# Loading the query weights in four stepped pieces of 16, 16, 32 and 64 partitions

## The chip, the core and the metric

The kernel runs on one core of a Trainium2 chip. The metric is the device time of one execution in microseconds; the figure before is the median of three runs. A core has an on-chip memory (SBUF) of 128 partitions, 16 DMA engines that bring data from HBM, and the engines TensorE (PE), VectorE (DVE), ScalarE (ACT), GpSimd (POOL) and SyncE (SP). SP issues nearly all loads here. Below, one of the 16 DMA engines is called a lane.

## What is computed

One token goes through a layer norm, attention against a cache of 16384 keys in each of 8 key heads (32 query heads, 128 wide), and a small gated network behind it:

```python
def _A_ref(x, k_cache, v_cache, wq, wo):
    q = (x @ wq).reshape(B, Sq, Hq, Dh).transpose(0, 2, 1, 3)
    k = jnp.repeat(k_cache, rep, axis=1)
    v = jnp.repeat(v_cache, rep, axis=1)
    p = softmax(jnp.einsum("bhqd,bhkd->bhqk", q, k) * (Dh ** -0.5))
    o = jnp.einsum("bhqk,bhkd->bhqd", p, v)
    return o.transpose(0, 2, 1, 3).reshape(B, Sq, Hq * Dh) @ wo
...
x = A_x
h = x + _A_ref(_layernorm(x), A_k_cache, A_v_cache, A_wq, A_wo)
h2 = h + _B_ref(_layernorm(h), B_w1, B_w2, B_w3, B_w4)
```

`wq` is 512 x 4096 and `wo` 4096 x 512 in bf16, 4 MB each; the keys and the values are 32 MB each. With a sequence of one token the shifted branch inside `_B_ref` sees zeros only, so that `w1` and `w2` are not read; `w3` and `w4` are.

## The kernel before

The program is written as a list of operations for each engine, in the order in which they are issued; a small planner puts a semaphore wait ahead of an operation whose data, named by keys such as `("v", 0)`, another engine or a load has to deliver. Nothing reorders the list.

Loads are made by `load` (L475), all on SP but that of the token, `x4`, which ACT issues. SP issues them in this order: the query weights `wq`; the keys of the first pair of heads (8 MB); then, each as its buffer comes free, values and keys of the pairs in turn, the last pair's keys in two halves; the output weights `wo`; the weights `w3` and `w4` in four loads; at the end the store of the output. A load of 128 partitions brings one contiguous row of HBM to each partition: 32 KB for `wq` and `wo`, 64 KB for a pair's keys or values.

`wq` is put into the buffer `vb`, which later holds the values, under the key `("v", 0)`. Ahead of its use stand the layer norm's operations on DVE. The last of these, at L630, writes the normalised token `xn`; it waits for `wq` as well, so that the matmuls behind it need to wait for `xn` alone:

```python
dve(lambda e: e.tensor_scalar(xn[:, :], hT[:, :, 0], st[0][:, 0:1], st[0][:, 6:7], ALU.add, ALU.mult),
    r=["hT", (("st", 0), 0), (("st", 0), 6)] + [("v", x) for x in range(VP)], w=["xn"])
```

At L639 PE multiplies `xn` with `wq` in 32 matmuls, one bank of 512 columns after the other. DVE transposes the queries (L646), puts them into `qb` (L653) and copies the pair's part to `qn` (L768). From then on the loop over the four pairs runs: DVE transposes the keys in pieces (L663), PE forms the scores (L674), a softmax follows (L688 to L706), and PE multiplies with the values (L722). Behind the last pair come the output weights (L809), the second layer norm and the network (L832, L858).

The load of the first values reuses `vb`, so that SP waits ahead of it until PE has read `wq`. The load of the next pair's keys waits until DVE has transposed the pair that lay in its buffer. At the end the matmuls at L809 wait for `wo`, and those at L858 for the pieces of `w4`.

Of the kernel before, what the change touches and what calls it, by code (L numbers as in the profile page):

```python
# [350 lines left out]
HQ = 32  # L351
HKV = 8
SK = 16384
DH = 128
REP = HQ // HKV
FM = 1792
NCH = D // 128
FQ = FM // 4
NHC = FM // 128

WO = ((0, 32),)
VP = 1

# [24 lines left out]
def bass_sequential_preLN__gqa_block_cached__mixer_s_mlp__decode_kernel(  # L388
# [13 lines left out]
    with ExitStack() as ctx:  # L402
# [26 lines left out]
        st = [sb(f"st{i}", [128, 16], FP32) for i in range(2)]  # L429
        added = sb("added", [128, 2], FP32)  # L430
        sti = [sb(f"sti{i}", [128, 2, 2], I32) for i in range(2)]
        xn = sb("xn", [128, NCH], BF16)
# [20 lines left out]
        wq_sb, wo_sb = vb, kb[2]  # L453
# [10 lines left out]
        hT = kt[:, 2944:3200].bitcast(FP32).rearrange("p (k u) -> p k u", k=NCH)  # L464
# [9 lines left out]
        def load(name, dst, src, key, by="SP", also=()):  # L474
            P.op(by, lambda e: e.dma_start(dst, src), w=[key, *also], dma=name)  # L475
# [4 lines left out]
        def load_keys(j, y):  # L480
            n = 128 * DH
            if j in WHOLE:
                load("k0", kb_all[:, AT[j] * n:(AT[j] + 2) * n], pair_rows(A_k_cache, j), ("r", AT[j], 0),
                     also=[("r", AT[j] + z, i) for z in range(2) for i in range(1 - z, RPARTS)])
                return
            load(f"half{y}", kb[y][:, :], pair_rows(A_k_cache, j)[:, y * n:(y + 1) * n], ("r", y, 0),
                 also=[("r", y, i) for i in range(1, RPARTS)])
# [19 lines left out]
        def act(fn, r=(), w=(), bank=(), own=None):  # L507
            return P.op("ACT", fn, r, w, bank, own=own)
# [15 lines left out]
        def unread_held(times, at):  # L524
            for _ in range(times):
                P.op("PE", lambda e: held(e, O_ps[1][at:, :], field[:, 0:128 - at], field[:, 0:512], True, True),
                     r=["qb"], bank=[("O", 1)])
# [9 lines left out]
        def piece(cuts, m):  # L537
            return [lo <= m < hi for lo, hi in cuts].index(True)
# [54 lines left out]

        load("x4", x4[:, :], A_x[0, 0:1, :].rearrange("o (q j) -> (o q) j", q=4), "x4", "ACT")
        wq_in = A_wq.rearrange("(p k) c -> p (k c)", k=NCH)
        load("wq", wq_sb[:, 0:NCH * HQ * DH], wq_in[:, :], ("v", 0), also=[("v", x) for x in range(1, VP)])
        load_keys(0, 0)

        dve(lambda e: e.memset(mean4[:, :], -1.0 / (32 * D)), w=["mean4"])
        for n in range(2):  # L600
# [8 lines left out]
            r=["ident_f", "x4"], w=["quarter"])  # L609
# [9 lines left out]
            r=["ident_f"], w=["row32"])  # L619
        dve(lambda e: e.tensor_reduce(maskdd[:, :], ident_f[:, :].rearrange("p (n d) -> p d n", d=4), AX.X, ALU.add),  # L620
            r=["ident_f"], w=["maskdd"])
# [3 lines left out]
        for z, src, key, of, n in ((zo, row32[:, :].rearrange("p (g n h) -> p g h n", g=2, h=REP), "zo", "row32", 4),  # L625
# [3 lines left out]
                src.unsqueeze(3).to_broadcast([128, 2, REP, 4, n]), AX.X, ALU.add), r=[of], w=[key])  # L629
        dve(lambda e: e.tensor_scalar(xn[:, :], hT[:, :, 0], st[0][:, 0:1], st[0][:, 6:7],  # L630
                                      ALU.add, ALU.mult),
            r=["hT", (("st", 0), 0), (("st", 0), 6)] + [("v", x) for x in range(VP)], w=["xn"])

        keys = [("s", 0), ("s", 1), ("O", 0), ("O", 1), "A", "mn", "spare0", "spare1"]
        wq_k = wq_sb[:, 0:NCH * HQ * DH].rearrange("p (k c) -> p k c", k=NCH)
        for i, key in enumerate(keys):
            P.part("query", i)
            for k in range(NCH):
                pe(lambda e, k=k: e.matmul(row[:, bass.ds(P.b + P.b0, 512)], copies(xn[:, k:k + 1], 128),  # L639
                                           wq_k[:, k, bass.ds(P.c + P.c0, REP * DH)], start=(k == 0), stop=(k == NCH - 1)),  # L640
                   r=["xn"], also=[("v", x) for x in range(VP)], w=["n" if key == "mn" else key], bank=[key])
        P.part()
        for g in range(2):
            half = banks[64 * g:64 * g + 64, PAIRS * g:PAIRS * g + PAIRS, :].rearrange("p j c -> p (j c)")
            for b in range(2):
# [3 lines left out]
                    r=["n" if x == "mn" else x for x in keys[PAIRS * g:PAIRS * g + PAIRS]], w=["qcol"],  # L649
                    bank=keys[PAIRS * g:PAIRS * g + PAIRS])  # L650
        for a in range(4):
            lo, hi, at = 32 * a, 32 * a + 32, QPAD + 32 * a
# [137 lines left out]
        act(lambda e: e.activation(scr[0:1, 1:2], mean4[0:1, 0:1], ACTF.Gelu_apprx_tanh), r=["mean4"], w=["scr"])  # L790
        for n, (lo, hi) in enumerate(WO):
            load(f"wo{n}", wo_sb[:, lo * D:hi * D], A_wo.rearrange("(p r) c -> p (r c)", p=128)[:, lo * D:hi * D],
# [5 lines left out]
        for n, (lo, hi) in enumerate(W4):  # L798
# [4 lines left out]
            r=["o_m"], w=["o_f"])  # L803
# [3 lines left out]
        for r_ in range(32):  # L807
# [3 lines left out]
                                              stop=(r_ < 4 or r_ >= 28), skip_group_check=(r_ >= 4)),  # L811
               r=[("r", 2, piece(WO, r_)), "o_b"], w=[("O", 0)], bank=[("O", 0)])
        unread_held(2, 96)
        h_ps, hkey = banks[:, 6, :], "spare0"
        for n in range(2):
            dve(lambda e, n=n: e.tensor_copy(osum[:, 256 * n:256 * n + 256], O_ps[0][:, 256 * n:256 * n + 256]),  # L816
                r=[("O", 0)], w=[("osum", n)], bank=[("O", 0)])
        for q in range(4):
            pe(lambda e, q=q: e.matmul(h_ps[32 * q:32 * q + 32, 0:128], copies(row32[:, 0:1], 32),  # L819
                                       osum[:, q * 128:(q + 1) * 128], start=True, stop=True),  # L820
               r=[("osum", q // 2), "row32"], w=[hkey], bank=[hkey])
# [4 lines left out]
            r=["hT", (S, 0)] + [("r", 0, 0)], w=["hc"])  # L826
# [3 lines left out]
        for k in range(NCH):  # L830
            for q in range(4):
                pe(lambda e, k=k, q=q: e.matmul(s_ps[32 * q:32 * q + 32, 0, 0:FQ], hc[:, k, :],  # L832
                                                w3_sb[:, k, q * FQ:(q + 1) * FQ], start=(k == 0), stop=(k == NCH - 1)),
                   r=["hc"] + [("r", 0, n) for n in (piece(W3, k),) if n], w=[("s", 0)], bank=[("s", 0)])
# [5 lines left out]
            r=["xs", (S, 6), "hr"], w=[hkey], bank=[hkey])  # L840
# [8 lines left out]
        for m in range(NHC):  # L849
# [5 lines left out]
            for o in range(4):  # L855
# [5 lines left out]
                   r=[("r", 0, len(W3) + piece(W4, m)), ("hcol", piece(GELU, m))],  # L861
                   w=[hkey], bank=[hkey])
# [7 lines left out]
             r=[("fin", 0), ("fin", 1)], w=["out"], dma="out")  # L870
# [32 lines left out]
```

## Time and profile before

| what | value |
|---|---|
| median of 3 runs | 189.37 us (189.31 to 189.54) |
| the profiled execution's own time | 189.73 us |
| its span, first to last instruction | 188.3 us |
| mean granted TensorE clock | 0.927 |
| HBM read | 79.17 MB |
| busy share of the span: PE, DVE, ACT, POOL | 70%, 62%, 7%, 2% |

The times of the views count from the first instruction of the span. The profiled execution took 1.43 us more than its span; that lies before the first and behind the last instruction. In the view of the DMA queues a stretch is cut into 40 equal slices. The line `DMA` gives the busy share in tenths and the line `GB/s` the bytes that were moved, and both put a packet wholly into the slice in which it begins; where slices are shorter than a packet takes, a number other than 0 marks a packet's beginning. `q1` is SP's queue and `q10` ACT's.

### The profile page before, as it was taken

To read this page: it belongs to the slowest core of one execution; us is meant where nothing else is said; L and a number is where in the kernel's file an instruction comes from. 1 tells how busy PE (TensorE), PEld (TensorE's weight loads), DVE (VectorE), ACT (ScalarE), POOL (GpSimd) and SP (SyncE) were. 2 spreads that over 40 slices of the span, in tenths; PEclk is the share of its full clock that TensorE was granted. 3 is DMA by queue.
4 is the path that set the end of the run, shared out by engine and by line. 5 is a ranking of instruction groups with operands and counts; after the bars stand their busy time and mean duration, and the time that the engine had idled before them with its cause. 6 is when DMAs were issued, how large, how long until landed. Compare 5 with 4: busy or idle time off the path is not lost.

```text
span 188.3 us, 2390 instructions
## 1 busy us (share of the span) xinstructions
PE 131.2 (70%) x768; PEld 50.0 (27%) x758; DVE 116.1 (62%) x141; ACT 13.8 (7%) x22; POOL 4.6 (2%) x8
## 2 busy tenths in 40 slices
PE   0109900579979913998979309899799989796774
PEld 0103300223322501333324103333235433232221
DVE  5730570999736008999363069994699898633155
ACT  3000200000004000000040000000310000410012
POOL 8100000000000000000000000000000000000000
PEclk9999995589999985599999975999999999999999
DMA  6999999999999999899999999998999999889994
GB/s 223 446 446 446 446 446 446 446 446 446 446 446 432 446 446 432 376 404 404 404 446 446 446 446 446 446 446 369 418 439 446 543 446 432 376 369 418 415 412 158
DMA packets 2175, 79.19 MB, mean 421 GB/s; under 512 B 254, under 2 KB 382, under 8 KB 510
## 3 DMA queue, kind: packets, MB, share of 16 engines
q1 hardware_dynamic: 2166, 79.17, 97.6%
q8 instruction: 1, 0.02, 0.0%
q10 hardware_dynamic: 8, 0.00, 0.0%
HBM read 79.17 MB, written 0.00 MB: 420 GB/s over the span
## 4 chain that ended last, share of the span: by engine, by line
DMA 66%; DVE 22%; PE 10%; issue 1%; SPq 0%; DVEq 0%
DMA kb<-in_A_k_cache_dram 48%; DVE kt L663 19%; DMA kb<-in_A_wo_dram 18%; PE banks L520 3%; PE banks L674 2%; PE banks L722 2%; PE banks L809 1%; DVE mx L688 1%; PE banks L858 1%; DVE kt L846 0%; PE banks L819 0%; SPq L475 0%; PE banks L691 0%; DVE kt L816 0%; PE banks L558 0%
## 5 line engine op out<-in xcount | busy, mean ns | idle before, releaser
L674 PE MATMUL banks<-kt,qn 128*128 x256 | 70.3, 413 | 31.3 <-DVE kt L663 30.3
L663 DVE STREAM_TRANSPOSE kt<-kb 128x2048 int32<-128x2048 int32 (+2 forms) x24 | 70.6, 2994 | 26.6 <-DMA kb<-in_A_k_cache_dram 25.3
L674 PEld LDWEIGHTS banks<-kt,qn 128*128 x256 | 26.1, 102 | 75.5 <-issue 62.4
L520 PE MATMUL banks<-qb 128*128 128x512 bf16 x71 | 26.3, 387 | 0.6
L722 PE MATMUL banks<-vb,pt 128*32 128x512 bf16 x256 | 14.7, 379 | 0.2 <-POOLq L501 0.2
L700 ACT ACTIVATE kt<-banks,bias 128x1024 bf16<-128x1024 f32 x4 | 4.5, 1113 | 132.5 <-DVE nmh L695 132.5
L639 PE MATMUL banks<-vb,xn 128*128 x32 | 9.2, 460 | 7.0 <-DVE xn L630 7.0
L520 PEld LDWEIGHTS banks<-qb 128*128 128x128 bf16 x71 | 6.9, 97 | 19.0 <-issue 18.6
L688 DVE TENSOR_REDUCE mx<-banks 128x1 f32<-128x1024 f32 x4 | 4.9, 1225 | 10.5 <-PE banks L674 10.5
L722 PEld LDWEIGHTS banks<-vb,pt 128*32 128x32 bf16 x256 | 8.6, 97 | 4.5 <-POOLq L501 0.3
L706 DVE STREAM_TRANSPOSE pt<-kt 64x1024 bf16<-64x1024 bf16 x6 | 7.4, 1239 | 3.3 <-ACT kt L700 3.2
L646 DVE STREAM_TRANSPOSE kt<-banks 64x1024 f32<-64x1024 f32 x4 | 4.8, 1227 | 7.4 <-PE banks L639 7.4
L639 PEld LDWEIGHTS banks<-vb,xn 128*128 128x128 bf16 x32 | 3.7, 115 | 12.2 <-issue 9.8
L683 ACT ACTIVATE banks<-mean 128x1024 f32<-128x1024 f32 x4 | 4.1, 1027 | 19.6 <-DVE kt L646 19.5
L691 PE MATMUL banks<-mxd,mean 128*128 128x128 f32 x8 | 2.0, 326 | 4.7 <-DVE mxd L689 4.7
L746 DVE SCALAR_TENSOR_TENSOR od<-banks,rowc,od 128x128 f32<-128x128 f32 x12 | 4.2, 351 | 0.4
L610 PE MATMUL banks<-x,quarter 4*128 4x128 bf16 x1 | 0.3, 282 | 5.4 <-DVE quarter L608 5.4
L816 DVE COPY kt<-banks 128x256 f32<-128x256 f32 x2 | 0.8, 420 | 5.0 <-PE banks L809 5.0
L608 DVE CAST quarter<-ident_f 4x128 bf16<-4x128 f32 x1 | 2.9, 2876 | 1.3 <-DMA x<-in_A_x_dram 1.3
L532 PE MATMUL banks<-qb 128*128 128x512 bf16 (+1 forms) x10 | 3.6, 379 | 0.0
L743 DVE TENSOR_SCALAR od<-banks,rowc 128x128 f32<-128x128 f32 x4 | 1.3, 318 | 3.7 <-PE banks L722 3.7
L751 PE MATMUL banks<-od,zo 128*32 128x128 f32 x10 | 2.0, 283 | 1.9 <-DVE od L746 1.6
(76 smaller groups left out, 44.3 us busy)
## 6 DMA issues: line engine op xcount, KB each, us to landing
kb<-in_A_k_cache_dram SPq DMA_DIRECT2D x2, 4096.0 KB, 31.6
vb<-in_A_wq_dram SPq DMA_DIRECT2D x1, 4096.0 KB, 12.5
kb<-in_A_wo_dram SPq DMA_DIRECT2D x1, 4096.0 KB, 33.8
kb<-in_B_w_dram SPq DMA_DIRECT2D x1, 1792.0 KB, 34.0
kb<-in_B_w_dram SPq DMA_DIRECT2D x1, 1152.0 KB, 36.4
kb<-in_B_w_dram SPq DMA_DIRECT2D x1, 512.0 KB, 37.2
kb<-in_B_w_dram SPq DMA_DIRECT2D x1, 128.0 KB, 37.1
vb<-in_A_v_cache_dram SPq DMA_DIRECT2D x4, 24.3
```

What stands on the lines that cost most here:

```text
L520: P.op("PE", lambda e: e.matmul(O_ps[1][:, :], field[:, 0:128], field[:, 0:512], start=True, stop=True), r=["qb"], bank=[("O", 1)], times= ...
L532: return e.add_instruction(mybir.InstMatmult(name=nc.get_next_instruction_name(), engine=m.engine, ins=m.ins, outs=m.outs, start_tensor_ca ...
L639: pe(lambda e, k=k: e.matmul(row[:, bass.ds(P.b + P.b0, 512)], copies(xn[:, k:k + 1], 128), wq_k[:, k, bass.ds(P.c + P.c0, REP * DH)], sta ...
L646: dve(lambda e, g=g, b=b, half=half: e.transpose(qcol[64 * g:64 * g + 64, 2 * b:2 * b + 2, :, :].rearrange("p e m u -> p (e m u)"), half.r ...
L663: P.op("DVE", lambda e, t=t, n=n: e.transpose(pieces(kt, t, n).bitcast(I32), pieces(kb[at], t, n).bitcast(I32)), r=[("r", at, i) for i in ...
L674: pe(lambda e, n=n: e.matmul(row[:, bass.ds(P.y, 512)], qn[:, n, bass.ds(P.q, 128)], key_piece(P.k, n), start=False, stop=(n == 3), skip_g ...
L683: act(lambda e: e.activation(s_all, copies(mean4[:, 0:1], 1024), ACTF.Identity, scale=0.0), r=["mean4", "p"], w=[("s", 0), ("s", 1)], **both)
L688: dve(lambda e: e.tensor_reduce(mx[:, :], s_all, AX.X, ALU.max), r=[("s", 0), ("s", 1)], w=["mx"], **both)
L700: act(lambda e: e.activation(p_sb[:, :], s_all, ACTF.Exp, bias=bias[:, 0:1], scale=float(SCALE), accum_out=acc[:, :]), r=[("s", 0), ("s", ...
L706: dve(lambda e, g=g, lo=lo, hi=hi: e.transpose(pt[lo:hi, :, :, g, :], p_sb[lo:hi, :]), r=["p"], w=["pt"])
L722: pe(lambda e, l=l, ct=ct, ch=ch: e.matmul(O_ps[0][32 * ct:32 * ct + 32, :], pt[:, l, ch, :, :].rearrange("p g u -> p (g u)"), tiles[:, l ...
L746: dve(lambda e, block=block, c=c: e.scalar_tensor_tensor(od[:, :], block, rowc[:, c:c + 1], od[:, :], ALU.mult, ALU.add), r=[key, "rowc", ...
```

## The change

```diff
+ROWS = ((0, 8), (4, 8), (2, 4), (1, 2))
 WO = ((0, 32),)
 VP = 1
...
         wq_in = A_wq.rearrange("(p k) c -> p (k c)", k=NCH)
-        load("wq", wq_sb[:, 0:NCH * HQ * DH], wq_in[:, :], ("v", 0), also=[("v", x) for x in range(1, VP)])
+        for n, (at, step) in enumerate(ROWS):
+            load("wq", wq_sb[at:128:step, 0:NCH * HQ * DH], wq_in[at:128:step, :], ("wq", n) if n else ("v", 0))
         load_keys(0, 0)
...
-            r=["hT", (("st", 0), 0), (("st", 0), 6)] + [("v", x) for x in range(VP)], w=["xn"])
+            r=["hT", (("st", 0), 0), (("st", 0), 6), ("v", 0)] + [("wq", n) for n in range(1, len(ROWS))], w=["xn"])
```

The 128 partitions of `wq` are loaded by four loads instead of one. The first takes partitions 0, 8, 16 and so on to 120, the second 4, 12 to 124, the third 2, 6 to 126, the fourth the 64 odd ones. Each row stays one contiguous run of 32 KB, and each partition receives what it received before. All four count up one semaphore, and the operation that makes `xn` waits until it has counted all four, with one wait as before.

On SP the loads at the head of the program stood in this order, with the partitions and the elements of each behind its names (`vb` takes `wq` first and the values later, `kb` the keys; `d_` marks the semaphore of a load, `e_` that of an engine):

```order
L475 DMA vb<-in_A_wq_dram 128x16384 [waits barrier_Pool_Activation_PE_DVE_SP_release]
L475 DMA kb<-in_A_k_cache_dram 128x32768
L475 DMA vb<-in_A_v_cache_dram 128x32768 [waits e_PE,e_DVE,d_wq]
L475 DMA kb<-in_A_k_cache_dram 128x32768 [waits e_DVE,d_k0]
L475 DMA vb<-in_A_v_cache_dram 128x32768 [waits e_PE,e_POOL_v,d_v]
```

and now, with all lines of the file one further down:

```order
L476 DMA vb<-in_A_wq_dram 16x16384 [waits barrier_Pool_Activation_PE_DVE_SP_release]
L476 DMA vb<-in_A_wq_dram 16x16384
L476 DMA vb<-in_A_wq_dram 32x16384
L476 DMA vb<-in_A_wq_dram 64x16384
L476 DMA kb<-in_A_k_cache_dram 128x32768
L476 DMA vb<-in_A_v_cache_dram 128x32768 [waits e_PE,e_DVE,d_wq]
```

The first keys are issued behind four loads instead of one; nothing else on SP has moved, and the rows of PE, DVE, ACT and POOL are the same.

## The prediction

> **What bounds the kernel now.** I read the chain that ended last first, since it says which kind of work the end hangs on. By engine and by line, in shares of the span:
>
> ```profile
> DMA 66%; DVE 22%; PE 10%; issue 1%; SPq 0%; DVEq 0%
> DMA kb<-in_A_k_cache_dram 48%; DVE kt L663 19%; DMA kb<-in_A_wo_dram 18%; PE banks L520 3%; PE banks L674 2%; PE banks L722 2%; PE banks L809 1%; DVE mx L688 1%; PE banks L858 1%; DVE kt L846 0%; PE banks L819 0%; SPq L475 0%; PE banks L691 0%; DVE kt L816 0%; PE banks L558 0%
> ```
>
> Two thirds are transfers, but the 22% of DVE could be read as a second limit. So I asked for the stretches between the landings on that chain; the last two columns are the busy share of the 16 lanes and the rate.
>
> ```profile
> 5.00:12.00 7.00, 0.87 (x3) 0.60 (x3) 4.83 (x21) 0.00 (x0) 0.32 (x1) 1.00 0.96 417
> ...
> 13.30:32.60 19.30, 9.21 (x32) 3.67 (x32) 6.18 (x10) 1.03 (x1) 0.00 (x0) 0.90 1.00 435
> 32.60:71.30 38.70, 28.15 (x150) 10.79 (x150) 22.53 (x14) 2.23 (x3) 0.00 (x0) 0.90 1.00 434
> 71.30:110.00 38.70, 29.13 (x150) 11.03 (x150) 24.10 (x21) 2.23 (x3) 0.00 (x0) 0.89 1.00 434
> 110.00:177.80 67.80, 57.34 (x314) 21.31 (x308) 50.50 (x49) 4.92 (x7) 0.00 (x0) 0.95 0.99 426
> ```
>
> The lanes are full from the query weights' landing to that of `wo`, and nearly so before (the first row; a rate there counts a packet where it begins). The DVE pieces of the chain only set when the next load is issued, and that load then queues behind others: the chain in order of time shows 8.84 us of transposes and then 29.72 us from an issue to its landing, while the lanes worked on without a gap.
>
> ```profile
> 0.73 0.40 SPq L475
> 1.13 0.05 issue
> 1.18 31.41 DMA kb<-in_A_k_cache_dram
> ...
> 32.67 8.84 DVE kt L663 x3
> ...
> 41.57 29.72 DMA kb<-in_A_k_cache_dram
> ...
> 144.07 33.76 DMA kb<-in_A_wo_dram
> 177.83 0.04 issue
> 177.87 1.94 PE banks L809 x32
> ```
>
> So the kernel is one queue of bytes. It starts at about 1.75 us, hands over `wo` at 177.83 us, and a tail of dependent work follows to the end. Whatever the first 4 MB cost more or less moves every later landing, and the end, by the same amount.
>
> How this queue starts is what the change touches. The view of the queues up to 3.5 us, in slices of 0.0875 us:
>
> ```profile
> GB/s 0 0 0 0 0 0 0 0 0 0 0 0 0 0 0 0 0 0 6 3 2247 749 749 377 0 0 0 374 374 374 0 374 0 0 0 0 0 374 0 0
> q1 hardware_dynamic: 16, 0.52, 49.3%
> q10 hardware_dynamic: 8, 0.00, 0.2%
> ```
>
> `q1` has begun 16 packets, 0.52 MB: one row of 32 KB in each lane. The first begin in the slice at 1.75 us and eleven by 2.1; four follow between 2.36 and 2.8, and the last lane comes at 3.24. The second rows, from 3.4 us in slices of 0.035 us:
>
> ```profile
> GB/s 0 0 0 936 0 1872 0 1872 0 936 936 936 936 0 0 3745 0 936 0 0 936 0 0 0 0 0 0 0 0 0 936 0 0 0 0 0 0 0 936 936
> ```
>
> Sixteen begin between slice 3 (3.5 us) and slice 30 (4.45 us); the last is ten slices, 0.35 us, behind the last but one, and 0.95 us behind the first. The load ends with the same picture: from 12.0 us in slices of 0.0325 us, sixteen lanes write their semaphore and begin the keys,
>
> ```profile
> GB/s 2017 2017 2016 0 4033 0 2017 2017 2017 2016 0 0 4033 4033 2017 0 0 2017 0 0 0 0 0 0 0 0 0 0 2017 0 0 0 0 0 0 0 0 0 0 0
> ```
>
> and the last does so in slice 28, eleven slices or 0.36 us behind the one before. A lane keeps its lag, and a load has landed when its slowest lane is done.
>
> **The change part by part.** The bytes, the rows and the readers stay. What is added:
>
> Three more issues on SP. One costs 0.45 us from start to start (0.73 to 1.18 in the chain), so the first keys go out at about 1.18 + 3 x 0.45 = 2.53 us. Behind them stands the first values' load:
>
> ```profile
> 0.73 0.40 SPq L475 DMA_DIRECT2D vb<-in_A_wq_dram  x1
> 1.18 0.42 SPq L475 DMA_DIRECT2D kb<-in_A_k_cache_dram  x1
> 23.39 0.33 SPq L475 DMA_DIRECT2D vb<-in_A_v_cache_dram  x1
> ```
>
> That one waits for PE until 23.39, so SP has 20 us to spare, and the lanes need the keys only when the weights are through, at about 12 us. Nor do the lanes run dry between the pieces: 4096 KB at 434 GB/s are 9.66 us, or 1.21 us for each of a lane's eight rows, and the next piece comes after 0.45. I take 0; if this cover failed, three issues would cost 1.35 us at most. The semaphore writes of the added loads, three for each lane, are far too small to time here: 0.
>
> One wait on DVE that counts to four loads instead of one. It is the wait that ends at 13.29 us, and only what makes queries stands behind it:
>
> ```profile
> 13.29 0.29 DVE L630 TENSOR_SCALAR xn<-kt,st 128x4 bf16<-128x4 f32 x1 [2.36 <-DMA vb<-in_A_wq_dram]
> ...
> 26.64 0.32 DVE L768 COPY qn<-qb 128x624 bf16<-128x624 bf16 x1
> 32.67 2.31 DVE L663 STREAM_TRANSPOSE kt<-kb 128x2048 int32<-128x2048 int32 x1 [5.70 <-DMA kb<-in_A_k_cache_dram]
> ```
>
> After `qn` DVE is idle for 5.70 us until the first keys land. If weights and keys are late by the same amount, this slack stays; it is used up only if the weights alone come 5.7 us late.
>
> The start of the lanes. A load of 16 rows can give each lane its row after an eighth of the rows that the one load lists. Bounds: nothing, if the stagger has another cause; 0.35 us, if the last lane only joins the others; 0.95 us, if all lanes run level with the first.
>
> Where the sixteen rows under way lie. This is the largest term, and the trace does not show it. ACT's load of the token has 4 rows and left 8 packets on `q10`, so with one semaphore write for each lane in use it ran on 4 lanes: a short load is dealt out row by row, whatever partitions it goes to. So load one puts partitions 0, 8, 16 to 120 into the sixteen lanes at once, load two 4, 12 to 124, and the later ones again spread all lanes over every eighth partition, if each lane gets neighbouring rows of its load. In the rows above a lane moves 434 / 16 = 27.1 GB/s whatever it carries, weights, keys or values, so the ceiling lies in the lane or in its way into SBUF, not in what is read. If it is the lane, the stepping costs 0. If it is the way, and rows eight apart share ways, the least that sharing can be is two lanes on one: each row then takes 2.42 us, and the 4 MB cost another 9.66 us. With only the two loads of 16 rows so hit, it is a quarter of that, 2.4 us.
>
> [...]
>
> Between 0 and 9.66 I take 9.66. The one load runs at the ceiling in every row, which a fixed match of lanes and ways explains, and the stepped loads would lose such a match. [...]
>
> Sum against the profiled execution: 189.73 + 9.66 = 199.4 us. It lay 0.36 us above the median of 189.37, so against that 199.0 us. This is one for one: `xn` moves from 13.3 to 23.0, `qn` to 36.6, the first keys' landing from 32.6 to 42.3, `wo` from 177.8 to 187.5, and each keeps its slack.
>
> **The rivals.**
>
> Faster. No ways are shared, and the short first load lets the last lane begin with the others. Its place is the first 3.3 us; it decides as soon as that lane begins its row before about 2.9 us and no row takes longer. For it speaks the lone lane at 3.24, whose lag of 0.35 us is still there when the load ends; against it, that eleven lanes started within 0.35 us although all 128 rows were listed at once. 189.37 - 0.35 = 189.0, down to 188.4 with all lanes level.
>
> Partly slower. Only the 16-row loads collide, because the longer ones are dealt to lanes as the 128 rows are: 189.37 + 2.4 = 191.8. The rows do not tell this from the full case.
>
> No change. Nothing is shared and the stagger comes from something that any first load meets, such as its first reads: the lane at 3.24 stays late. 189.4, within 0.2% (0.38 us), about the least that a measurement here can tell from no change. The even 434 GB/s afterwards fits this as well as it fits the forecast.
>
> **How the numbers follow.** Full sharing: 0.48. Partial sharing, or a smaller cost from issues that are not hidden: 0.13. Faster by over 0.2%: 0.27, since the late lane is plain in the trace but its gain stands or falls with the first question. Within 0.2%: 0.12. So slower 0.61. The predicted time is that of full sharing, 199.0 us; by itself it would lie between 198.1, with the best start (0.95 us), and 200.0, if lanes that are still at the weights hold up others' first keys by most of a row's 1.21 us. As cases of both signs are likely, the range reaches from 188.7, which leaves out the better part of the faster case, to 200.0.
>
> **What would show it.** Full sharing: a rate of about 217 GB/s between 5 and 20 us, `xn` near 23 us, the first keys landed near 42, all later stretches at 434. Partial: a low rate over the first 5 us alone, keys at 35. Faster: 16 first packets without a straggler at 3.2 us, 417 GB/s or more from 5 to 12 us, keys near 32.2. The forecast is wrong if the rate does not fall while `wq` comes in; the step that failed is then that of the ways into SBUF.

## The result and the profile after

The changed kernel takes 192.03 us (median of 4 runs, 192.03 to 192.19), the kernel before 189.45 us (median of 4): 1.0135 times as long, 95% interval 1.0118 to 1.0153, or 2.58 us more. The profiled execution took 192.19 us, 2.46 more than that of before.

The chain in order of time (start, duration, what) has the shape of before; the first keys land at 35.06 us instead of 32.59, and `wo` at 180.30 instead of 177.83:

```profile
0.73 0.60 SPq L476
...
3.27 31.79 DMA kb<-in_A_k_cache_dram
...
35.14 8.84 DVE kt L665 x3
...
180.30 0.04 issue
180.35 1.94 PE banks L811 x32
```

2.47 us later at the first landing, 2.47 at the last, 2.46 at the end: all of it arises while the weights come in, and it is handed through unchanged. The stretches behind show the queue as full as before:

```profile
35.10:73.80 38.70, 29.03 (x150) 10.95 (x150) 22.53 (x14) 2.23 (x3) 0.00 (x0) 0.90 1.00 434
73.80:112.50 38.70, 28.40 (x150) 10.85 (x150) 24.10 (x21) 2.23 (x3) 0.00 (x0) 0.90 1.00 434
```

The head of the queue can be read row by row. For that I cut the stretches so that each holds the beginnings of one row of 32 KB in all sixteen lanes. Rate times length, divided by 32,768 bytes, is then 16, and the DMA share (last but one column) times the length is the mean time of a row. Of the kernel before, the first two rows and the last:

```profile
1.70:3.30 1.60, 0.00 (x0) 0.00 (x0) 0.79 (x1) 1.10 (x2) 1.60 (x1) 1.00 1.08 328
3.50:4.50 1.00, 0.00 (x0) 0.00 (x0) 1.00 (x1) 0.00 (x0) 1.00 (x2) 1.00 1.21 524
...
10.70:11.80 1.10, 0.00 (x0) 0.00 (x0) 0.22 (x1) 0.00 (x0) 0.00 (x0) 1.00 1.10 477
```

1.73 us for the first row (1.08 x 1.60), 1.21 for each behind it. Of the changed kernel, all eight rows:

```profile
2.10:3.30 1.20, 0.00 (x0) 0.00 (x0) 1.15 (x1) 0.70 (x2) 1.20 (x1) 1.00 1.82 437
3.90:5.30 1.40, 0.00 (x0) 0.00 (x0) 1.40 (x1) 0.00 (x0) 1.40 (x1) 1.00 1.71 375
6.20:7.70 1.50, 0.58 (x2) 0.50 (x2) 1.06 (x6) 0.00 (x0) 0.00 (x0) 1.00 1.26 350
8.40:9.20 0.80, 0.00 (x0) 0.00 (x0) 0.69 (x5) 0.00 (x0) 0.00 (x0) 1.00 1.52 655
9.70:10.40 0.70, 0.00 (x0) 0.00 (x0) 0.70 (x2) 0.00 (x0) 0.00 (x0) 1.00 1.75 749
10.90:11.60 0.70, 0.00 (x0) 0.00 (x0) 0.03 (x1) 0.00 (x0) 0.00 (x0) 1.00 1.74 749
12.10:12.90 0.80, 0.00 (x0) 0.00 (x0) 0.00 (x0) 0.00 (x0) 0.00 (x0) 1.00 1.52 655
13.30:14.10 0.80, 0.00 (x0) 0.00 (x0) 0.00 (x0) 0.00 (x0) 0.00 (x0) 1.00 1.52 655
```

The first row takes 2.18 us, the second 2.39, the third 1.89, and from the fourth on 1.22. The first row, of the first load of 16, holds the start as well and is 0.45 us longer than before. The second, of the other load of 16, is about twice as long. The third, with which the load of 32 begins while some lanes are still at their second, is half way, and the rest of the loads of 32 and 64 runs at full speed. Against the rows of before that is 0.45 + 1.18 + 0.68 = 2.31 us. In the trace the last lane's semaphore write for the weights also comes 2.31 us later, at 15.24 us instead of 12.93; most of the remaining 0.16 us passes between a load's last semaphore write and the end of the wait for it (0.47 us at the first keys, 0.34 before). The start, in slices of 0.0875 us, has moved too:

```profile
GB/s 0 0 0 0 0 0 0 0 0 0 0 0 0 0 0 0 0 0 6 6 0 0 0 0 1872 1123 749 374 0 0 374 749 0 374 0 0 0 374 0 0
```

The first rows begin at 2.1 us instead of 1.75. The first load's issue takes SP 0.60 us instead of 0.40 (first line of the chain), which covers 0.20 of these 0.35 us; the rest is not explained. The last row again begins at 3.24, but its lag is lost in the disturbed rows: the fourth rows all begin within 0.8 us, where the second rows of before took 1.0.

### The profile page after: what moved, and what is told of

It is laid out like the page before. It is cut to its first block, busy times and chain, and to the rows that moved or that the text cites. A ratio compares the mean times of both kernels' runs of the same rounds, so it can differ in the third digit from the quotient of the medians.

```text
span 190.7 us, 2393 instructions
## 1 busy us (share of the span) xinstructions
PE 129.8 (68%) x768; PEld 49.5 (26%) x758; DVE 116.5 (61%) x141; ACT 13.8 (7%) x22; POOL 4.6 (2%) x8
## 4 chain that ended last, share of the span: by engine, by line
DMA 66%; DVE 21%; PE 10%; SPq 1%; issue 1%; DVEq 0%
DMA kb<-in_A_k_cache_dram 48%; DVE kt L665 18%; DMA kb<-in_A_wo_dram 18%; PE banks L521 3%; PE banks L676 2%; PE banks L724 2%; SPq L476 1%; PE banks L811 1%; DVE mx L690 1%; PE banks L860 1%; DVE kt L848 0%; PE banks L821 0%; PE banks L693 0%; DVE kt L818 0%; PE banks L559 0%
## 5 line engine op out<-in xcount | busy, mean ns | idle before, releaser
L676 PE MATMUL banks<-kt,qn 128*128 x256 | 69.6, 410 | 32.7 <-DVE kt L665 31.6
L641 PE MATMUL banks<-vb,xn 128*128 x32 | 8.4, 430 | 9.5 <-DVE xn L632 9.5
```

Source lines behind the costliest of these rows:

```text
L676: pe(lambda e, n=n: e.matmul(row[:, bass.ds(P.y, 512)], qn[:, n, bass.ds(P.q, 128)], key_piece(P.k, n), start=False, stop=(n == 3), skip_g ...
```

## The experiments

My theory after the result was that two lanes meet on one way into SBUF in the loads of 16 rows alone (sharing). Its rivals: each added load costs about the same (count); a short first load starts the lanes badly (start); the rows 256 KB apart collide in HBM. What the traces show is how long a row takes; that lanes share ways into SBUF is a reading of those times. Each experiment is the changed kernel with another `ROWS`, unless it says otherwise.

**Two loads of 64 rows**

```diff
-ROWS = ((0, 8), (4, 8), (2, 4), (1, 2))
+ROWS = ((0, 2), (1, 2))
```

> The query weights in two loads of 64 rows at steps of 2. Sharing (two lanes meet on one way into SBUF in the loads of 16 rows alone): nothing collides, 189.0 to 189.6 us, keys landed near 32.3 to 32.9. Sharing with neighbouring rows dealt to each lane in longer loads too: 199 us. Count (each added load costs a third of the measured 2.58 us, 0.86): 190.3 us.

189.78 us against 189.56 of before, 1.0015 times (1.0005 to 1.0025). The second row of this kernel takes 2.02 x 0.60 = 1.21 us:

```profile
3.90:4.50 0.60, 0.00 (x0) 0.00 (x0) 0.60 (x1) 0.00 (x0) 0.60 (x1) 1.00 2.02 874
```

**Three loads of 32, 32 and 64 rows**

```diff
-ROWS = ((0, 8), (4, 8), (2, 4), (1, 2))
+ROWS = ((0, 4), (2, 4), (1, 2))
```

> Three loads of 32, 32 and 64 rows at steps of 4, 4 and 2: the two loads of 16 become one of 32, the rest stays. Sharing: the whole 2.5 us are gone, 189.0 to 189.6 us, every packet 1.21 us from the second row on. Count: two added loads, 191.2 us. Start (a short first load starts the lanes badly): between, 190 to 191 us.

189.76 us, 1.0010 times (1.0001 to 1.0020). The first two rows of this kernel:

```profile
2.00:3.20 1.20, 0.00 (x0) 0.00 (x0) 1.04 (x1) 0.79 (x2) 1.20 (x1) 1.00 1.56 437
3.90:4.50 0.60, 0.00 (x0) 0.00 (x0) 0.60 (x1) 0.00 (x0) 0.60 (x1) 1.00 2.03 874
```

The second row takes 2.03 x 0.60 = 1.22 us. In both runs the cost has all but gone with the loads of 16, although one or two loads are added. Both are slightly over the 189.6 that sharing gave, and their intervals stay below what count (190.3 and 191.2) and start (190 to 191) gave. So the rows of loads of 32 and 64 stepped rows run without a collision, at 1.22 and 1.21 us; with neighbouring rows for each lane, all lanes would again have stood eight partitions apart, as in the loads of 16. Which row goes to which lane, no run shows.

**Eight loads of 16 rows**

```diff
-ROWS = ((0, 8), (4, 8), (2, 4), (1, 2))
+ROWS = ((0, 8), (4, 8), (2, 8), (6, 8), (1, 8), (5, 8), (3, 8), (7, 8))
```

> Eight loads of 16 rows, all at steps of 8. Sharing: all eight rows of a lane take 2.42 us, 189.4 + 9.7 = 199.1 us, about 217 GB/s from 5 to 20 us. Count: seven added loads at 0.86 us, 195.5 us. Start: 192.0 us, as with four loads.

198.87 us, 1.0485 times (1.0467 to 1.0504), 9.3 us more. The second and the last row:

```profile
4.20:5.10 0.90, 0.00 (x0) 0.00 (x0) 0.90 (x1) 0.00 (x0) 0.90 (x1) 1.00 2.68 583
...
18.40:19.50 1.10, 0.00 (x0) 0.00 (x0) 0.00 (x0) 0.00 (x0) 0.00 (x0) 1.00 2.18 477
```

2.41 and 2.40 us: the doubling does not wear off over eight rows. No load, two and eight of 16 rows cost 0.2, 2.6 and 9.3 us more than before, about 1.2 to 1.3 us each.

**The four loads in the opposite order**

```diff
-ROWS = ((0, 8), (4, 8), (2, 4), (1, 2))
+ROWS = ((1, 2), (2, 4), (4, 8), (0, 8))
```

> The same four loads in the opposite order: 64, 32, 16, 16 rows. Sharing: the doubled rows now come last, 191.5 to 192.1 us, the low rate stands at about 9 to 14 us instead of the beginning. Start: the cost is gone with the short first loads, 189.4 us. Count: 192.0 us with no stretch of low rate after the start.

192.23 us, 1.0138 times (1.0120 to 1.0156). Row two, six, seven and eight:

```profile
4.00:4.40 0.40, 0.00 (x0) 0.00 (x0) 0.40 (x1) 0.00 (x0) 0.40 (x1) 1.00 3.05 1311
...
8.90:9.20 0.30, 0.00 (x0) 0.00 (x0) 0.30 (x2) 0.00 (x0) 0.00 (x0) 1.00 4.04 1748
10.10:10.50 0.40, 0.00 (x0) 0.00 (x0) 0.40 (x1) 0.00 (x0) 0.00 (x0) 1.00 5.09 1311
12.00:12.70 0.70, 0.00 (x0) 0.00 (x0) 0.00 (x0) 0.00 (x0) 0.00 (x0) 1.00 3.46 749
```

1.22 and 1.21 us while the long loads run, then 2.04 and 2.42 for the two of 16. The cost goes with these loads to the end of the weights, so it is not the start.

**Two halves of 64 neighbouring partitions**

```diff
-ROWS = ((0, 8), (4, 8), (2, 4), (1, 2))
+ROWS = ((0, 64), (64, 128))
...
-    load("wq", wq_sb[at:128:step, ...], wq_in[at:128:step, :], ...)
+    load("wq", wq_sb[lo:hi, ...], wq_in[lo:hi, :], ...)
```

> Two loads of 64 rows as the first run's, but partitions 0 to 63 and then 64 to 127. [...] Sharing that hangs on the number of rows in a load alone: 189.8 us, as with two loads at steps of 2. An unstepped load is also to show whether its issue on SP takes 0.4 us, as the one load's, or 0.6, as the stepped ones'.

199.96 us, 1.0549 times (1.0534 to 1.0564). The second row:

```profile
3.80:5.10 1.30, 0.00 (x0) 0.00 (x0) 1.30 (x1) 0.00 (x0) 1.30 (x1) 1.00 1.97 403
```

2.56 us a row. As many loads with as many rows as in the first experiment, and only the choice of rows, and with it of partitions, differs: 189.78 against 199.96. So it is not the number of rows in a load. The rows of the stepped loads of 64 took 1.21 us. The two issues took 1.18 us together here as well, about as long each as the stepped ones, so that is not due to the step:

```profile
0.73 1.18 SPq L476 DMA_DIRECT2D vb<-in_A_wq_dram  x2
```

**The same destinations, the source in order**

```diff
-ROWS = ((0, 8), (4, 8), (2, 4), (1, 2))
+ROWS = ((0, 8, 0), (4, 8, 16), (2, 4, 32), (1, 2, 64))
...
-    load("wq", wq_sb[at:128:step, ...], wq_in[at:128:step, :], ...)
+    load("wq", wq_sb[at:128:step, ...], wq_in[first:first + 128 // step, :], ...)
```

> The changed kernel's four loads with the same destinations, but the rows of wq are read in order, 0 to 15, 16 to 31, 32 to 63, 64 to 127; the partitions then hold the wrong rows of the weights, of the same size. Sharing on the way into SBUF: the two loads of 16 still double, 192.0 us. Collision in HBM between rows 256 KB apart: the loss goes, 189.5 us.

191.53 us, 1.0107 times (1.0092 to 1.0122). The first four rows:

```profile
2.10:2.50 0.40, 0.00 (x0) 0.00 (x0) 0.34 (x1) 0.40 (x1) 0.40 (x1) 1.00 4.93 1311
3.60:4.50 0.90, 0.00 (x0) 0.00 (x0) 0.90 (x1) 0.00 (x0) 0.90 (x1) 1.00 2.62 583
6.00:6.90 0.90, 0.44 (x2) 0.44 (x2) 0.69 (x5) 0.00 (x0) 0.00 (x0) 1.00 1.90 583
7.90:8.40 0.50, 0.00 (x0) 0.00 (x0) 0.41 (x3) 0.00 (x0) 0.00 (x0) 1.00 2.43 1049
```

1.97, 2.36, 1.71 and 1.22 us: with neighbouring rows of HBM the second row still doubles. Of the half microsecond that this kernel is faster than the changed one, 0.21 lie in the first row and 0.18 in the third; its lanes begin closer together. So the doubling does not hang on the step between the rows in HBM; with the same partitions it stays (2.36 us), which speaks for a collision on the side of SBUF.

**Eight blocks of 16 neighbouring partitions**

```diff
-ROWS = ((0, 8), (4, 8), (2, 4), (1, 2))
+ROWS = tuple((lo, lo + 16) for lo in range(0, 128, 16))
...
-    load("wq", wq_sb[at:128:step, ...], wq_in[at:128:step, :], ...)
+    load("wq", wq_sb[lo:hi, ...], wq_in[lo:hi, :], ...)
```

> Eight loads of 16 neighbouring partitions. [...] If each eight neighbours had one way: eight lanes on each, 8 x 8.5 = 68 us more, 257 us. If neighbours had ways of their own: 189.8 us.

215.59 us, 1.1379 times (1.1360 to 1.1398). A row of the middle:

```profile
17.90:19.50 1.60, 0.00 (x0) 0.00 (x0) 0.00 (x0) 0.00 (x0) 0.00 (x0) 1.00 2.84 328
```

4.54 us, 3.7 times the 1.21 of the one load's rows, and 26 us more in all. One way for each eight neighbours (257 us) and one for each partition (189.8) are ruled out.

**Steps of 7**

```diff
-ROWS = ((0, 8), (4, 8), (2, 4), (1, 2))
+ROWS = tuple((at, 112, 7) for at in range(7)) + ((112, 128, 1),)
...
-    load("wq", wq_sb[at:128:step, ...], wq_in[at:128:step, :], ...)
+    load("wq", wq_sb[at:to:step, ...], wq_in[at:to:step, :], ...)
```

> Seven loads of 16 rows at steps of 7 (partitions 0, 7 to 105, then 1, 8 to 106 and so on), then 112 to 127 as one block. [...] If any load of 16 rows doubles whatever its partitions: about 220 GB/s between 4 and 9 us, 198.9 us or more, as with eight loads at steps of 8.

198.72 us, 1.0496 times (1.0469 to 1.0523): near the 198.9 us of loads of 16 rows that double whatever their partitions. The rate was 315 GB/s from 4 to 6.5 us and 236 from 6.5 to 9, against the 220 of that case. The third, the fifth and the eighth row, of the loads from partitions 2 and 4 and of the block:

```profile
5.60:7.10 1.50, 0.72 (x3) 0.50 (x2) 0.93 (x6) 0.00 (x0) 0.00 (x0) 1.00 1.48 350
...
9.90:10.70 0.80, 0.00 (x0) 0.00 (x0) 0.80 (x2) 0.00 (x0) 0.00 (x0) 1.00 2.09 655
...
15.30:16.90 1.60, 0.00 (x0) 0.00 (x0) 0.00 (x0) 0.00 (x0) 0.00 (x0) 1.00 2.34 328
```

2.22, 1.67 and 3.74 us on the mean of sixteen rows. The second, the sixth and the seventh row took 2.04, 2.02 and 2.22 us, the fourth 1.82. Lane by lane, the trace has no packet of the third row under 2.01 us and none of the fifth under 1.57. So it is not that some lanes take 2.42 us and the others 1.21: in these two rows all are slowed. While some lanes are still at one load others are at the next, so a lane can also meet one of another load; what that adds is not separated, and the cause is open. The time equals that of eight loads at steps of 8, but the rows do not: they take 1.67 to 2.22 us at steps of 7 and 3.74 in the block, against 2.40 there.

**Steps of 4 in the middle**

```diff
-ROWS = ((0, 8), (4, 8), (2, 4), (1, 2))
+ROWS = tuple((at, 96, 4) for at in range(32, 36)) + ((0, 32, 1), (96, 128, 1))
...
-    load("wq", wq_sb[at:128:step, ...], wq_in[at:128:step, :], ...)
+    load("wq", wq_sb[at:to:step, ...], wq_in[at:to:step, :], ...)
```

> Four loads of 16 rows at steps of 4 in the middle (partitions 32, 36 to 92, then 33, 37 to 93 and so on), then 0 to 31 and 96 to 127 as blocks of 32. [...] If a load of 16 rows doubles whatever its partitions: all eight rows at 2.4 us, 199 us.

196.68 us, 1.0365 times (1.0342 to 1.0388), under the 199 us of loads of 16 rows that double whatever their partitions. The second row, and a stretch with the third:

```profile
3.60:4.40 0.80, 0.00 (x0) 0.00 (x0) 0.80 (x1) 0.00 (x0) 0.80 (x1) 1.00 1.54 655
4.80:6.50 1.70, 0.32 (x2) 0.14 (x2) 1.29 (x6) 0.00 (x0) 0.52 (x1) 1.00 1.08 347
...
14.90:17.00 2.10, 0.00 (x0) 0.00 (x0) 0.00 (x0) 0.00 (x0) 0.00 (x0) 1.00 1.21 250
```

The second row takes 1.54 x 0.80 = 1.23 us: here a load of 16 rows ran at full speed. So 16 rows in a load do not double by themselves. The last row, of a block of 32 neighbours, takes 2.54. But the stretch with the third holds 18 rows (347 GB/s x 1.70 us) of 1.63 us on the mean, although its load, too, is of 16 rows at steps of 4, which sharing does not explain. In the trace four of the sixteen lanes have no row under way at 5.5 us, the last of them until 6.45, while the three rows that begin at 4.88 to 5.14 us take 2.27 to 2.42. Why is open.

**The keys issued later.** The kernel before; the first keys' load is moved on SP's list and made to wait until `pt` has been zeroed, by naming `pt` as something that it reads:

```diff
-            P.op(by, lambda e: e.dma_start(dst, src), w=[key, *also], dma=name)
+            P.op(by, lambda e: e.dma_start(dst, src), r=behind, w=[key, *also], dma=name)
...
+                     behind=[] if j else ["pt"],
...
-        load_keys(0, 0)
...
         pool(lambda e: e.memset(pt[:, :, :, :, :], 0.0), w=["pt"])
+        load_keys(0, 0)
```

> The kernel before with one edit: the first keys' load is issued behind the zeroing of pt, at about 5.3 us instead of 1.2, while the lanes have weights until 12 us. If the listing of the keys is what keeps one lane from starting before 3.2 us: no straggler, 189.45 - 0.35 = 189.1 us. If the straggler comes from the listing of the weights' 128 rows: unchanged, 189.45 us.

189.53 us against 189.50, 1.0000 times (0.9991 to 1.0008). In the profile the straggler of 3.24 us is gone, and the first keys land at 5.34 + 26.88 = 32.22 us instead of 32.59, but `wo` at 144.00 + 33.79 = 177.79, only 0.04 us earlier:

```profile
GB/s 0 0 0 0 0 0 0 0 0 0 0 0 0 0 0 0 0 0 0 12 1872 1498 1123 374 374 0 0 0 749 0 0 0 0 0 0 0 0 0 0 0
```

```profile
5.34 26.88 DMA kb<-in_A_k_cache_dram
...
144.00 33.79 DMA kb<-in_A_wo_dram
```

The 0.37 us are given back on the way, and the times of the semaphore writes in the two traces tell where. The last lane is ahead of that of before by 0.35 us at 109 us (109.24 against 109.59), by 0.20 at 129, by 0.08 at 148, and level at 168 (167.72 against 167.69). The lanes have hardly a gap there, 0.02 us each, so the transfers themselves took longer; why is open. These are one profile of each kernel; the runs show no gain.

## Why the prediction was right or wrong

The time moved the way that was forecast, but by 2.58 us where 9.66 were forecast.

- *The queue is the bound, and the head's cost reaches the end one for one*: right for a head that costs more, 2.47 us at the first keys, 2.47 at `wo`, 2.46 at the end. For one that costs less the runs do not bear it out: with the keys issued later, 0.37 us at the first keys became 0.04 at `wo` and nothing at the end.
- *Two lanes on one way, a row at 2.42 us*: right in price for lanes eight partitions apart; the ways themselves no run shows. The changed kernel's second row took 2.39 us, those of eight loads of 16 took 2.40, and that kernel, at 198.87 us, stands where the forecast stood.
- *The later loads again spread all lanes over every eighth partition, if each lane gets neighbouring rows of its load*: this step failed. The condition was an assumption about dealing that no row bore out, and it carried six of the eight rows. A row of before even spoke against it: dealt in neighbours, the one load would have put its sixteen lanes at partitions 0, 8 to 120 too, and its rows, at 1.21 us, would have doubled like those of the loads of 16. So the sentence that the rows do not tell partial from full sharing was wrong as well. Loads of 32 and 64 stepped rows take 1.21 us a row, as the one load's rows do; the term was 2.4 us by the forecast's own price for the two loads of 16, and measured 2.58, not 9.66. No run shows 9.66 us for these four loads; the nearest, eight loads of 16, cost 9.3. The rival "partly slower" named this condition, gave 191.8 us and the first keys at 35 (35.06 were measured), and had 0.13 of the chance with other small costs.
- *Faster by a better start*: the straggler's lag did go, in the changed kernel by its fourth row. It brought nothing: the first rows begin 0.35 us later, and where the lag was removed without that (the keys issued later) the end stayed as well.
- *Issues on SP cost nothing*: their price was low, 0.62 us from start to start instead of 0.45. Behind the first one they are hidden, as said; the first rows begin later. With no load of 16 the two kernels are 0.2 us over before, near what can be measured. Their profiles do not show where: the first keys land at 32.56 and 32.65 us, against 32.59 before.
- *No change*: excluded by the interval.

## What to carry to other kernels

Where loads bound a kernel, ask which partitions the lanes fill at the same moment, not only how many bytes and loads there are: the same 4 MB in two loads took 189.8 us at steps of 2 and 200.0 us as two halves. Loads of 32 and 64 rows at steps of 4 and 2 ran as fast, row for row, as one of 128 (1.22 and 1.21 us); loads of 16 rows at steps of 8 did not (2.40). When a forecast hangs on how the hardware deals out work, price each way of dealing, and give the part that a row of the trace bears out (a short load, row by row) more weight than its extension to longer loads. Ask also what the assumption would do to the kernel as it stands: here the one load's rows would have answered it.

## What was not expected

The loads of 16 rows at steps of 7 took neither 1.21 nor 2.42 us a row but 1.67 to 2.22 on the mean, where those at steps of 8 took 2.40; why is open. The rows of the blocks of 16 neighbours took 4.54 us, 3.7 times 1.21; why that much is open too. And the first issue took 0.40 us for 128 rows, but 0.54 to 0.60 for 64 rows, neighbouring or stepped, and for 16 or 32 stepped ones, with the first row 0.3 us later; why is open. Eight blocks of 16 neighbours began at 1.75 us, as the 128 rows did:

```profile
GB/s 0 0 0 0 0 0 0 0 0 0 0 0 0 0 0 0 0 0 0 12 1498 1498 2621 374 0 0 0 0 0 0 0 0 0 0 0 0 0 0 0 0
```
